# Keeping the pieces of a folded weight in on-chip memory, and a new instruction order

## The chip, the cores and the metric

The kernel runs on one core of a Trainium2 chip. The core has a matrix engine (TensorE, PE; its weight loads are PEld), a vector engine (VectorE, DVE), a scalar engine (ScalarE, ACT), GpSimd (POOL) and SyncE (SP). In this kernel SP does nothing but issue DMAs. SBUF is the on-chip memory that all engines read, PSUM holds matmul results. The metric is the device time of one execution in microseconds, as a median over runs.

## The reference

Three stages follow each other.

```python
# attention, q, k, v: [2, 8, 768, 64], proj: [64, 6]
q_bucket = sum over bits of ((q @ proj) > 0) * 2**bit        # k_bucket the same
scores = where(q_bucket == k_bucket, q @ k.T / sqrt(64), -1e9)
attn = exp(scores - max) / (sum + 1e-9)
x = (attn @ v) as [1536, 512]
# layer 1, d_ff 2048
g = s * relu(x @ w_in)**2 + b
x = g @ w_out
# layer 2, d_ff 1024
h = ((x @ w1) * (x @ w2)) @ w3
out = h @ w_out
```

## The kernel before, in words

All matmuls work on numbers split into a high and a low part in a reduced fp32 format, and take three matmuls (high x high, low x high, high x low), so groups of PE come in threes.

**Attention.** There are 16 heads of 768 queries. `begin` loads q and k of a head, stacked, as t (head 0 in two halves of 384 columns, at L344; others whole, at L347) and v as tv (L348). `q1` is the high part of q and k, `k2` the low part (L395; L456 for head 0). `bits` (L492) multiplies with the projection pj, `mm` (L510) turns the signs into +1 and -1; `q2` and `k1` are rows of q, k and mm copied to other partitions, by a DMA (L381, L466, L477) or, in part for head 0, by a cast (L434 on ScalarE, L436 on VectorE, L437 on GpSimd). Score products `sc` (L529) hold scores and a penalty for each differing bit. VectorE takes the row maxima (L543), ScalarE the exponentials p (L551), PE transposes them (t, L565), ScalarE, VectorE and GpSimd split the transposes into pt (L586 to L607), and PE multiplies with v (o, L571 and L572). L674 and lines near it normalise. `warm` at L502 is a matmul whose result nobody reads; the counts of these groups are in FILLS.

**Layer 1** runs beside attention and behind it: h = x @ w_in, rl and g on ScalarE and VectorE (L828 to L842), then x = g @ w_out, in quarters of d_ff, for both halves of the tokens. Each weight arrives as raw (L717) and is split in six steps by VectorE, ScalarE and GpSimd (L257 to L271). The pieces are saved to DRAM (kept_wi, kept_wo; L737) and reloaded for the second half of the tokens (`again`, L747).

**Layer 2** first folds w3 @ w_out into one matrix whl (`fold`, tiles psw, L1162): for both halves of w3's columns, 8 pieces of w_out (wo2), and 8 of w3 with each. Weights w1 and w2 give seven products of a fast two-by-two scheme (p, L759), which VectorE combines (c, L1132) and multiplies; y (L1203) is the product with whl. Tiles of this stage lie in pools that are opened once attention's are closed; `w2` is the pool of the fold's pieces and of whl, with NW2 buffers of 4 KB a partition.

**What sets the order.** Functions record operations in `Plan` with what each reads and writes. Three tables of constants then fix everything: ORDER gives the order in which all operations are issued (two letters for one), WAYS the engine of each operation that has a choice, PLACES the buffer of each tile. Every engine runs its own operations in that order, and waits by semaphores for what they read and for the buffer that they write.

Of the kernel before, what the change touches and what calls it, by code (L numbers as in the profile page):

```python
# [1263 lines left out]
```

## Time and profile before

| | before |
|---|---|
| median of 3 runs (us) | 741.36 (741.2 to 744.16) |
| the profiled execution (us) | 742.74 |
| its span, first to last instruction (us) | 740.9 |
| PE busy | 729.0 us, 98% |
| VectorE busy | 590.8 us, 80% |
| ScalarE busy | 393.2 us, 53% |
| GpSimd busy | 297.5 us, 40% |
| DMA traffic | 163.03 MB, mean 220 GB/s |

The profile comes from one execution, which took 742.74 us in all; 740.9 of it are the span that the views cut up. Shares of busy time are means over stages with different limits, so stretches and waits say more than the totals.

### The profile page before, as it was taken

The page shows a single profiled execution, that of the slowest core. Times are in us where ns is not written, and L with a number is a line of the kernel's source. Part 1 is how long each engine was busy: PE and PEld are TensorE (multiplying, and loading weights), DVE is VectorE, ACT ScalarE, POOL GpSimd, SP SyncE. Part 2 cuts the span into 40 slices and gives each one's busy share as a digit, 9 for nine tenths or more (in the row PEclk, how much of TensorE's full clock was granted, in tenths as well). Part 3 has the DMA queues.
Part 4 walks back from the last instruction along what each step waited for, and adds up shares of the span by engine and source line. Part 5 has one row for each costly group of instructions (what it writes and reads, how often), then busy time and mean ns, then how long its engine had stood idle before and what let it go on. Part 6 is the DMA issues. An engine that isn't in the chain of part 4 may idle for free.

```text
span 740.9 us, 12707 instructions
## 1 busy us (share of the span) xinstructions
PE 729.0 (98%) x4356; PEld 694.6 (94%) x4356; DVE 590.8 (80%) x1133; ACT 393.2 (53%) x778; POOL 297.5 (40%) x322
## 2 busy tenths in 40 slices
PE   8899999999999999999999999999999999999997
PEld 6889999999999999999999998999998999999996
DVE  7999999999889889999898667665998965664542
ACT  6989989987667667665373432433533312311111
POOL 2698989886565564334230311032125200111000
PEclk9999999999999999999999999999999999999999
DMA  7856557566677477347888996788899998475502
GB/s 217 244 132 175 141 160 194 149 181 171 195 228 236 119 232 255 93 133 254 288 267 298 317 312 242 256 274 290 315 338 315 353 312 261 141 240 186 179 22 86
DMA packets 78592, 163.03 MB, mean 220 GB/s; under 512 B 8896, under 2 KB 46272, under 8 KB 78528
## 3 DMA queue, kind: packets, MB, share of 16 engines
q1 hardware_dynamic: 78528, 162.22, 68.5%
q8 instruction: 35, 0.57, 0.3%
q14 instruction: 29, 0.24, 0.1%
HBM read 103.09 MB, written 41.21 MB: 195 GB/s over the span
## 4 chain that ended last, share of the span: by engine, by line
PE 86%; DVE 7%; DMA 3%; ACT 2%; issue 1%; SPq 0%; DVEq 0%; ACTq 0%
PE x L759 18%; PE h L759 15%; PE p L759 15%; PE y L1203 9%; PE t L565 7%; PE sc L529 7%; PE psw L1162 6%; PE o L571 4%; PE o L572 4%; PE bits L492 2%; DVE sc L543 1%; DVE pt L607 1%; DMA t<-in_qkT 1%; DMA q<-mm 1%; DMA rd<-rq 1%
## 5 line engine op out<-in xcount | busy, mean ns | idle before, releaser
L759 PE MATMUL h<-x,w_wi 128*128 128x384 f32 x768 | 148.1, 338 | 0.0
L759 PE MATMUL x<-g,w_wo 128*128 128x384 f32 x768 | 146.9, 337 | 1.0 <-DVE rl L833 0.9
L759 PEld LDWEIGHTS x<-g,w_wo 128*128 128x128 f32 x768 | 133.6, 188 | 3.6 <-DVE rl L833 1.6
L759 PEld LDWEIGHTS h<-x,w_wi 128*128 128x128 f32 x768 | 133.6, 188 | 2.5 <-DVE pt L607 0.2
L1132 DVE TENSOR_TENSOR c<-c,p 128x384 f32<-128x384 f32 x112 | 60.2, 552 | 57.7 <-PE p L759 54.4
L543 DVE TENSOR_SCALAR_CACHE_REDUCE sc<-sc 128x768 f32<-128x768 f32 x96 | 91.6, 957 | 3.4 <-PE sc L529 2.4
L551 ACT ACTIVATE p<-sc,least 128x768 f32<-128x768 f32 x96 | 86.9, 906 | 11.1 <-DVE sc L543 7.7
L529 PE MATMUL sc<-k,q 128*128 128x384 f32 x384 | 87.0, 347 | 3.0 <-ACT p L551 2.0
L565 PE MATMUL t<-ident,p 128*128 128x128 f32 x576 | 83.9, 273 | 0.2
L759 PE MATMUL p<-x,w 128*128 128x384 f32 x384 | 77.5, 337 | 0.4 <-DVE c L1132 0.3
L571 PE MATMUL o<-pt,vv 128*128 128x256 f32 x288 | 76.9, 295 | 0.1
L572 PE MATMUL o<-pt,vv 128*128 128x256 f32 x288 | 73.1, 282 | 0.0
L565 PEld LDWEIGHTS t<-ident,p 128*128 128x128 f32 x576 | 67.9, 140 | 5.3 <-DVE pt L607 1.5
L759 PEld LDWEIGHTS p<-x,w 128*128 128x128 f32 x384 | 68.0, 188 | 4.5 <-DVE c L1132 1.3
L597 POOL TENSOR_TENSOR pt<-pf,pt 128x512 fp32r<-128x512 f32 x48 | 63.2, 1317 | 21.6 <-ACT pt L593 20.7
L607 DVE TENSOR_TENSOR pt<-t,pt 128x512 fp32r<-128x512 f32 x96 | 65.0, 683 | 6.7 <-ACT pt L603 5.5
L529 PEld LDWEIGHTS sc<-k,q 128*128 128x128 f32 x384 | 64.4, 188 | 5.2 <-ACT p L551 3.0
L603 ACT CAST pt<-t 128x512 fp32r<-128x512 f32 x96 | 56.0, 586 | 16.7 <-PE t L565 7.6
L571 PEld LDWEIGHTS o<-pt,vv 128*128 128x128 f32 x288 | 54.4, 189 | 0.8 <-DVE xf L624 0.3
L572 PEld LDWEIGHTS o<-pt,vv 128*128 128x128 f32 x288 | 54.5, 189 | 0.2
L838 ACT ACTIVATE g<-rl,b_bc 128x384 fp32r<-128x384 f32 x64 | 38.9, 615 | 25.5 <-PE x L759 17.4
L1162 PE MATMUL psw<-w_wo,w_w 128*128 128x512 f32 x192 | 51.6, 394 | 0.0
(263 smaller groups left out, 1271.7 us busy)
## 6 DMA issues: line engine op xcount, KB each, us to landing
w<-kept_s SPq DMA_DIRECT2D x64, 256.0 KB
kept_wo<-w_wo SPq DMA_DIRECT2D x24, 512.0 KB
w_wo<-kept_wo SPq DMA_DIRECT2D x24, 512.0 KB
w<-kept_a SPq DMA_DIRECT2D x48, 256.0 KB
raw_wi<-in_w_in SPq DMA_DIRECT2D x16, 512.0 KB
...
```

What stands on the lines that cost most here:

```text
L529: nc.tensor.matmul(sc()[:, i, :HALF], x[:, t], y[:, i * HALF : (i + 1) * HALF], start=st, stop=not st)
L543: lambda j=j, sc=sc: nc.vector.tensor_scalar(sc()[:, :, :HALF], sc()[:, :, :HALF], OUT, None, ALU.min, ALU.min, accum_out=least()[:, j : j ...
L551: lambda j=j, k=k, sc=sc: nc.scalar.activation(ps[j](), sc()[:, :, :HALF], AF.Exp, bias=least()[:, j : j + 1], scale=-1.0, accum_out=ssum( ...
L565: nc.tensor.transpose(tp()[:, e, j * P : (j + 1) * P], flat[:, c * P : (c + 1) * P], ident)
L571: nc.tensor.matmul(o()[:, :U], w, pt()[:, 0, e], start=(c == 0), stop=False)
L572: nc.tensor.matmul(o()[:, :U], w, pt()[:, 1, e], start=False, stop=(c == NC - 1))
L597: lambda pf=pf, pt=pt: nc.gpsimd.tensor_tensor(pt()[:, 1], pf(), r32(pt()[:, 0]), ALU.subtract),
L607: lambda tp=tp, pt=pt: nc.vector.tensor_tensor(pt()[:, 1], tp(), r32(pt()[:, 0]), ALU.subtract),
L759: nc.tensor.matmul(ps()[:, :n], x, y, start=(i == 0 and e == 0), stop=(i == len(terms) - 1 and e == 2))
L1132: "cadd", "dve", 0.47, rank, lambda: nc.vector.tensor_tensor(x(out), a(), p(), op), [(ps, 1), *reads], writes
L1162: nc.tensor.matmul(ps(), w3()[:, p, c], wo()[:, q], start=(j == 0 and e == 0), stop=(j == 7 and e == 2))
L1203: nc.tensor.matmul(y(), abt()[:, p, c], wt()[:, q], start=(i == 0 and e == 0), stop=(i == DF2 // P - 1 and e == 2))
```

## The change

Three things change.

1. In layer 2 the 8 wo2 pieces are no longer saved to DRAM in half 0 of the fold and reloaded in half 1; the list `wos` keeps them. The pool w2 grows from 14 to 17 buffers.
2. The memory that is set aside for descriptors of GpSimd's DMAs shrinks from 16 to 1 KB a partition, by an argument of the program's constructor.
3. ORDER, WAYS and PLACES are new. Among operations with a choice of engine, six normalisations (L674) and three sums of weights (L1092) go from VectorE to GpSimd. In the first microseconds, the split of the first half of head 0's t goes from ScalarE to VectorE, one cast to q2 from VectorE to GpSimd, another from ScalarE to GpSimd, and one cast to k2 from VectorE to ScalarE. The FILLS groups are 9, 6, 3 and 3 in both; before, the last three stand together.

All line numbers from 986 on are one lower in the changed kernel.

```diff
-NW2 = 14
+NW2 = 17
...
 ORDER = (
-    "AKAAAFABALAGBmXkAMACBnANADX0AEXsAOAbAWAPAVAcAhAXAfAdAUBoAgAQAeAYAZAjAaBvAiXlBuBpAkBwB0DPAqXmAlBsAmArAnB1BqAs"
...
+    "AKALAFABAMAGAABmXkBnANX0AOAVXsACAXAbADAEAfAhAWAPAcAgBoAUAdAYAQAZAeAiAaAjBpBuAkBvXlB0AqBwXmAlDPAnB1ArXnARAmAo"
...
-            whl = [None] * DJ
+            whl, wos = [None] * DJ, []
...
                 for j in range(DJ):
                     if half == 0:
-                        wo = piece(wo2[j // 2], f"wo2_{half}_{j // 2}", j % 2, r + step, late_raw, late_w, ("wo2", j))
-                    else:
-                        wo = again(f"wo2_{half}_{j // 2}", j % 2, ("wo2", j), late_w)
+                        wos.append(piece(wo2[j // 2], f"wo2_{half}_{j // 2}", j % 2, r + step, late_raw, late_w))
+                    wo = wos[j]
                     w3 = piece(w3T[half], f"w3_{half}", j, r - 5 * step, late_raw, late_w)
...
-    nc = bacc.Bacc("TRN2", target_bir_lowering=False, num_devices=1)
+    nc = bacc.Bacc("TRN2", target_bir_lowering=False, num_devices=1, dynamic_dma_scratch_size=1024)
```

Two places show how the order moves.

**The start of the program.** SP's first DMA rows before (t_0 is q and k of head 0, of which each row loads a half; numbers at the end of a name count the tiles):

```order
L344 DMA t_0_229<-in_qkT 128x384
L293 DMA pj_85<-in_projp 128x128
L344 DMA t_0_229<-in_qkT 128x384
L347 DMA t_1_255<-in_qkT 128x768
L717 DMA raw_wi_0_0_0_257<-in_w_in 128x1024
L348 DMA tv_0_259<-in_vl 128x384
L348 DMA tv_1_262<-in_vl 128x384
L717 DMA raw_wi_0_0_2_267<-in_w_in 128x1024
```

SP's first DMA rows now:

```order
L344 DMA t_0_221<-in_qkT 128x384 x2
L348 DMA tv_0_230<-in_vl 128x384
L293 DMA pj_85<-in_projp 128x128
L347 DMA t_1_249<-in_qkT 128x768
L717 DMA raw_wi_0_0_0_251<-in_w_in 128x1024
L348 DMA tv_1_253<-in_vl 128x384
L717 DMA raw_wi_0_0_2_257<-in_w_in 128x1024
L717 DMA raw_wi_0_0_1_263<-in_w_in 128x1024
```

The two halves of t_0 now stand together at the front; tv_0 and pj come behind them, and t_1 fourth as before, behind a tv.

VectorE's rows at the same place before, from the projection's split to the first step of a weight:

```order
L304 TENSOR_TENSOR pj_85<-pj_85,ones_232 128x128
L307 CAST pj_h_86<-pj_85 128x128
L309 TENSOR_TENSOR pj_l_87<-pj_85,pj_h_86 128x128
L456 SCALAR_TENSOR_TENSOR k2_0_272<-t_0_229,qs_71,q1_0_264 128x384
L436 CAST k1_0_275<-q1_0_264 64x384
L456 SCALAR_TENSOR_TENSOR k2_0_272<-t_0_229,qs_71,q1_0_264 128x384
L436 CAST q2_0_283<-q1_0_264 64x384
L510 TENSOR_SCALAR mm_0_291<-bits_0_0_277,thr_75,sgn_76 128x384
L510 TENSOR_SCALAR mm_0_291<-bits_0_1_287,thr_75,sgn_76 128x384
L436 CAST k2_0_272<-mm_0_291 64x384
L260 TENSOR_SCALAR raw_wi_0_0_0_257<-raw_wi_0_0_0_257 128x512
```

VectorE's rows now:

```order
L448 TENSOR_SCALAR q1_0_255<-t_0_221,qs_71 128x384
L456 SCALAR_TENSOR_TENSOR k2_0_259<-t_0_221,qs_71,q1_0_255 128x384
L304 TENSOR_TENSOR pj_85<-pj_85,ones_224 128x128
L307 CAST pj_h_86<-pj_85 128x128
L309 TENSOR_TENSOR pj_l_87<-pj_85,pj_h_86 128x128
L436 CAST k1_0_261<-q1_0_255 64x384
L456 SCALAR_TENSOR_TENSOR k2_0_259<-t_0_221,qs_71,q1_0_255 128x384
L510 TENSOR_SCALAR mm_0_282<-bits_0_0_274,thr_75,sgn_76 128x384
L510 TENSOR_SCALAR mm_0_282<-bits_0_1_284,thr_75,sgn_76 128x384
L395 SCALAR_TENSOR_TENSOR k2_1_303<-t_1_249,qs_71,q1_1_280 128x768
L260 TENSOR_SCALAR raw_wi_0_0_0_251<-raw_wi_0_0_0_251 128x512
```

The first half's split (q1_0) has come to VectorE, ahead of pj. The cast to q2_0, which stood between the second k2_0 and the first mm, and the cast of mm to k2_0 behind the second are gone from it. k2_1 now follows mm directly.

**The first folds, beside layer 1's x_0_2_1.** PE's rows before (h is the product with w_in, w_wo_1_0 a reloaded quarter of w_out, psw the fold; behind a row stands what it waits for, DMAHW3 being a DMA):

```order
L759 MATMUL h_0_3_3_5607<-x0_3_3032,w_wi_1_0_1_5274 128x384 x3
L759 MATMUL h_0_3_3_5607<-x0_3_3032,w_wi_1_0_2_5359 128x384 x3
L759 MATMUL h_0_3_3_5607<-x0_3_3032,w_wi_1_0_3_5384 128x384 x3
L759 MATMUL h_0_3_2_5600<-x0_3_3032,w_wi_1_0_1_5274 128x384 x3
L759 MATMUL h_0_3_2_5600<-x0_3_3032,w_wi_1_0_2_5359 128x384 x3
L759 MATMUL x_0_2_1_5653<-g_0_2_0_5509,w_wo_1_0_0_5563 128x384 [waits DMAHW3_49,DVE_49]
L759 MATMUL x_0_2_1_5653<-g_0_2_0_5509,w_wo_1_0_0_5563 128x384 x2
L759 MATMUL x_0_2_1_5653<-g_0_2_1_5515,w_wo_1_0_1_5440 128x384 x3
L1162 MATMUL psw_0_2_5670<-w_wo2_0_0_0_5336,w_w3_0_0_5521 128x512 x3
L759 MATMUL h_0_3_2_5600<-x0_3_3032,w_wi_1_0_3_5384 128x384 x3
```

PE's rows now:

```order
L759 MATMUL h_0_3_3_5588<-x0_3_2978,w_wi_1_0_2_5351 128x384 x3
L759 MATMUL h_0_3_1_5572<-x0_3_2978,w_wi_1_0_3_5366 128x384 x3
L759 MATMUL h_0_3_2_5595<-x0_3_2978,w_wi_1_0_1_5248 128x384 x3
L759 MATMUL h_0_3_3_5588<-x0_3_2978,w_wi_1_0_3_5366 128x384 x3
L759 MATMUL h_0_3_2_5595<-x0_3_2978,w_wi_1_0_2_5351 128x384 x3
L1161 MATMUL psw_0_2_5638<-w_wo2_0_0_0_5324,w_w3_0_0_5512 128x512 x3
L759 MATMUL h_0_3_2_5595<-x0_3_2978,w_wi_1_0_3_5366 128x384 x3
L759 MATMUL x_0_2_1_5653<-g_0_2_0_5495,w_wo_1_0_0_5541 128x384 [waits DMAHW0_49,DVE_49]
L759 MATMUL x_0_2_1_5653<-g_0_2_0_5495,w_wo_1_0_0_5541 128x384 x2
L759 MATMUL x_0_2_1_5653<-g_0_2_1_5502,w_wo_1_0_1_5424 128x384 [waits DMAHW4_49]
```

The fold psw_0_2 and the last group of h_0_3_2 have moved from behind the first rows of x_0_2_1 to in front of them.

SP's rows that lead up to the reloads for x_0_2_1, before:

```order
L747 DMA w_wo_1_0_1_5440<-kept_wo_0_0_1_158 128x1024
L747 DMA w_wo_1_0_2_5450<-kept_wo_0_0_2_159 128x1024
L737 DMA kept_wo2_0_0_0_185<-w_wo2_0_0_0_5336 128x1024
L717 DMA raw_wo2_0_1_1_5463<-in_wo2 128x1024
L737 DMA kept_wo_0_3_3_184<-w_wo_0_3_3_5142 128x1024
L914 DMA kept_t3_1_224<-t3_0_1_5481 256x1x384
L717 DMA raw_w3_0_1_5545<-in_w3T 128x1024
L747 DMA w_wo_1_0_3_5555<-kept_wo_0_0_3_160 128x1024
L747 DMA w_wo_1_0_0_5563<-kept_wo_0_0_0_157 128x1024
```

SP's rows now:

```order
L717 DMA raw_w3_0_0_5395<-in_w3T 128x1024
L737 DMA kept_wo_0_3_3_184<-w_wo_0_3_3_5135 128x1024
L747 DMA w_wo_1_0_1_5424<-kept_wo_0_0_1_158 128x1024
L717 DMA raw_wo2_0_1_1_5453<-in_wo2 128x1024
L717 DMA raw_w3_0_1_5532<-in_w3T 128x1024
L914 DMA kept_t3_1_216<-t3_0_1_5466 256x1x384
L747 DMA w_wo_1_0_0_5541<-kept_wo_0_0_0_157 128x1024
L747 DMA w_wo_1_0_2_5551<-kept_wo_0_0_2_159 128x1024
L747 DMA w_wo_1_0_3_5558<-kept_wo_0_0_3_160 128x1024
```

The save kept_wo2_0_0_0 is gone; w_wo_1_0_0 now stands ahead of w_wo_1_0_2 and w_wo_1_0_3, one load of raw_w3 and one kept_t behind the last save.

## Rows read from the trace of the kernel before

**Rows 1.** The page, part 1: engine, busy us (share of the span) xinstructions.
```profile
PE 729.0 (98%) x4356; PEld 694.6 (94%) x4356; DVE 590.8 (80%) x1133; ACT 393.2 (53%) x778; POOL 297.5 (40%) x322
```

**Rows 2.** Stretches of the span: each engine's busy us (xinstructions), granted clock, DMA share, GB/s.
```profile
0.00:15.00 15.00, 12.43 (x57) 10.92 (x58) 10.57 (x35) 9.27 (x18) 3.74 (x9) 1.00 0.81 243
15.00:30.00 15.00, 12.39 (x77) 10.15 (x76) 14.19 (x27) 13.55 (x27) 7.11 (x7) 1.00 0.69 195
...
90.00:150.00 60.00, 59.85 (x436) 57.37 (x435) 57.31 (x120) 55.23 (x117) 53.67 (x64) 1.00 0.60 165
...
400.00:525.00 125.00, 125.00 (x660) 117.21 (x659) 86.59 (x151) 44.86 (x78) 24.42 (x25) 1.00 0.83 285
525.00:600.00 75.00, 74.46 (x403) 70.08 (x402) 68.38 (x122) 29.74 (x55) 22.84 (x17) 1.00 0.97 335
```

**Rows 3.** Waits of PE: waiting line <- awaited line: us in total, times, longest.
```profile
PE sc L529 <- ACT p L551: 2.0, 2, 1.2
...
PE bits L492 <- DVE pt L607: 1.0, 1, 1.0
PE x L759 <- DVE rl L833: 0.9, 1, 0.9
...
PE p L759 <- DVE c L1132: 0.3, 1, 0.3
```

**Rows 4.** Timeline of 0 to 31 us: start, duration, engine, line, operation.
```profile
1.64 0.42 SPq L344 DMA_DIRECT2D t<-in_qkT  x1
...
5.90 0.61 ACT L451 ACTIVATE q<-t,qs 128x384 fp32r<-128x384 f32 x1 [2.03 <-DMA t<-in_qkT]
...
7.07 0.92 POOL L386 TENSOR_SCALAR q<-t,qs 128x768 fp32r<-128x768 f32 x1 [5.78 <-DMA t<-in_qkT]
7.20 1.01 DVE L436 CAST q<-q 64x384 fp32r<-64x384 f32 x1
...
7.37 0.38 PE L492 MATMUL bits<-k,pj_h 128*128 128x384 f32 x1
...
8.24 1.26 DVE L510 TENSOR_SCALAR mm<-bits,thr,sgn 128x384 fp32r<-128x384 f32 x2
...
10.26 1.01 DVE L395 SCALAR_TENSOR_TENSOR k<-t,qs,q 128x768 fp32r<-128x768 f32 x1
...
11.79 0.96 DVE L543 TENSOR_SCALAR_CACHE_REDUCE sc<-sc 128x768 f32<-128x768 f32 x1
...
12.83 2.25 PE L502 MATMUL warm<-pj_h 128*128 128x384 f32 x12
...
14.91 0.60 PE L565 MATMUL t<-ident,p 128*128 128x128 f32 x4
```

**Rows 5.** Timeline of 49.5 to 53.5 us, GpSimd and VectorE.
```profile
49.91 1.83 POOL L375 TENSOR_TENSOR k<-t,q 128x768 fp32r<-128x768 f32 x1
...
50.15 1.88 DVE L260 TENSOR_SCALAR raw_wo<-raw_wo 128x512 int32<-128x512 uint32 x1
```

**Rows 6.** Timeline of 372 to 392 us, SP's queue and PE.
```profile
382.47 0.80 SPq L747 DMA_DIRECT2D w_wo<-kept_wo  x2
...
390.76 0.93 PE L759 MATMUL x<-g,w_wo 128*128 128x384 f32 x4 [0.87 <-DVE rl L833]
```

**Rows 7.** Waits of SP's queue, 380 to 395 us.
```profile
SPq L747 <- DMA kept_wo<-w_wo: 1.6, 1, 1.6
```

**Rows 8.** DMA traffic of 375 to 392 us.
```profile
DMA packets 1810, 5.42 MB, mean 319 GB/s; under 512 B 171, under 2 KB 683, under 8 KB 1808
```

**Rows 9.** Groups by line and shape: xcount, busy us, mean ns, idle before.
```profile
L674 POOL TENSOR_TENSOR xf<-rb,xf 128x256 f32<-128x256 f32 x14 | 10.8, 772 | 6.5 <-DMA rb<-rd 6.4
...
L260 DVE TENSOR_SCALAR raw_wo<-raw_wo 128x512 int32<-128x512 uint32 x24 | 12.2, 508 | 1.6 <-DMA raw_wo<-in_wo 1.6
...
L674 DVE TENSOR_TENSOR xf<-rb,xf 128x256 f32<-128x256 f32 x10 | 4.6, 464 | 0.0
```

**Rows 10.** DMA queues: kind, packets, MB, share of 16 engines.
```profile
q1 hardware_dynamic: 78528, 162.22, 68.5%
```

More of the change, by code (lines that the diff above doesn't have):

```diff
@@ new lines @@
+    "AsBqX1ApXtAtX2BsXuA/X3BrXvBtAxAuA8BAAyBxA2EeA9BBByX4AzBUXoA+ASA0AvBzA3BRBVEfATX5DRA4AwXwXpBGDXDSA1BWDYA5BSXq"
+    "BHDTA6B2EgDUXxDVX8A7BTBCX6B3DaBbBDDWGIB5BIB4DQBEBLBJDbB6BFBMCTBcBNXyB7BgCUBXBhDcBKX9DZCVCWBiYMCAX+YUBYBOCXCB"
+    "X/B8BPCyCLBdBZCFCYBQBeCzBaC1B9YAC0BfC2EhBjCGDfEiEnB+C3EoCMCdDgBkDiCeDHL8BlDdElCCCHCZDhCDCNB/EmCOCiDjCaEjCoYB"
+    "D0YNEqDkCbYCCEEpCIEkCfD3D1CJErCgCjC4C8CKD2DICcCPDeCkChC9DJD4ClDKC5C+DBCmEJC6EsGKD5CnDpC/EKDCEMDqCpC7ELGLDDDA"
+    "CqDlYVDrCrDEGMENDmDuGJDFD+DnGRDvEvGSDGD/CQDwGNGTEOD6DsEwCsDoEtEyDLGOExEADtEzL+HYGPCRD7EDEBGQGUFME0D8GVDxCSFN"
@@ new lines @@
+    "AHEPDyETCtEEDzFPEUFEEFCwD9FOCuFQDMECEYEQGWEVHaEGYEFRERDNFrCxE5EZCvFsFuEHEWE6E1EIFtE+EaHbESFvEXDOE2HiEbE/HhE3"
+    "HcGZFwFAFWFFFSEcGaGcFXEuJCE7HdEdGbGdFhHfHZE8E4HkHgGuFTGXFGFbHeFHGYE9FUGeFBHlGvF6HjFYFcGxFCFdHmFZFxGwFDF1FiFV"
+    "GyJEF2FaFyHDFjF3GzFzFkFeGAHEF4GjFIFfHGF7FgGfHFGBJFF8F0F5AJGkHHFlJGF9GgGoJLGCF+GhHpJMHIF/GDG0FJHqGiGpKSFKG9G1"
+    "GqHsFLGlG2HrJHGmHtG4HnIGG5FmJIGnHuIHHoJJGEGrG+YFJOHJIIJKG6JNIJG/G7JPGsHNIKFnJDHSFpHOIlFoGtILH+YGG3JQHzXzImGF"
+    "HKG8H0YHHAKUHPH4FqHLHBIoHQHTH/HCHvInIAHUHMIBKVHRIpHwIQH5KWKcJTHxGGKbIqHVKdH6IMJUHWGHNMKZIRJWH1HXJVKaKXH2JXHy"
@@ new lines @@
+    "KeIVINI6KYH3IbJYJRJoIOKfJSISH7IcJpIvIWITJrH8IXIwI0H9IrJqYIICIPIdIUJsYJIsIeIYIxNOJ9ItIZKgIyI1JZI7AIIaJdJtL9I2"
+    "IuYKJ+IzJeIfKAJaJ/IDI3KTL/JbJiKBI4JuMAMGJjKjMFJfI5JyJkKCJcKkJgO2MBJvKmI8JwKlI9IgJhKnJ3IEKhYcLAJzIFMCKoJlLBJ0"
+    "MDJmKiKDJ4MIMELDI+IjJnK4LCIhKMJ5J1JxMJLEKHMHKELfIkKIKFIiJ2LFMKO4J6YLKJLgKtNNJ7LiKKKNJ8KpKuLjKGNPLVI/KLKqKOKy"
+    "NVLkJAK5KPYdLGJBK6KrKQK7MNLhKvLWKRLKNXNQMOKsKzNWMQLLK0MPLPMRKwQGNRLHMiNSMSMLKxLXMjLYK1MMLMNTK2LIMlLNLQNYNUMk"
+    "LlK3LpNZLRQILJK8LqMmLOL0LmLSLrYWLuLTNaM3LnLsMnLUMcM4LZLoYXMdM6LvYOMTM5MeO5LtLwMXMUO6O/M7LxMYPBMsPALyL1MxM8MV"
@@ new lines @@
+    "NdK9LzYsMZL2LaNeL3NgMtMaNbMWNhNfO7NcYtO8MyMbLbMzK+N6YPL4LcMuMfK/N7MoMgLdO9MvMpMhYuO+N8PCYvMqPDNGNiYYO3N9YQNB"
+    "YwMrL5NCYRYxMwPEN+M0LeNHYDYSM9M1OZNIN/M2NnNDaUOaNsM+RxNyOcNENoTAM/ObNjOdNAQJL6NFNtNJYeQPNkOENuL7NpPHNlNKNqOJ"
+    "OeNLOANzNmPIOFQKPKOKOjPJOLNrPLNvOkQLOGNwN0PcOBQMN1OPOHPFYkOCPMQQQNNxRwOoPdPGYyX7ODYZOIQOOuPfPeaVQTOQOMaWQROf"
+    "QSONPgOlYlQHOgYmOmN2aXOhPxOpOROOYnPhOSYaPyPWOiYoOnYfRyYpP0OqYqPNYgPXQUY0POacPYY1YhOvOrYzRzPRYrY2PSN3OwY3PPY8"
+    "P1YiOTY4Y9PzY+R7R0ZEOxN4OsQXQVP2aMOtY/Y5R6ZFOUPTQYQ0ZAPUY6ZBPrQZOyPQQ1ZGYbZCZMadR5PsY7ZHYjZDZNXrZIaNZOOVZJZP"
@@ L118 @@
+    "3124323o353p364M3q374933213r3825344N3s4O3t39273u3+4P3v4Q4T3w4R4U3x4i4V4j4W4k4X294Z4Y4B4b4c4e4d4f4l4g5W4m4p5l"
+    "4n4J4q4s4r4H4t4w4u564x4K5d4y4z4D6I4+4/5z435A445B3/5s455C5E465X40475F41485Y5G4F5Z5H4E425I5D5a5e5J5b5f5c4A5g5h"
+    "5O5p5i4C5j5k5P5q5m5r5n5t5o5u5w5v5x505y5153525457555K586C596D5+4G5/6P6A6Q6B5U6E6F5M6R4I6G6S6J6H6T6K6U5Q6L5S6M"
+    "5L6N6V6O6Z6a6W6l5R6h6m6b6i6c5V6f6g6n5N6o6r6X6s5T6Y6d6j6e6k6p6q"
 )
 WAYS = (
[L120 removed]
@@ new lines @@
+    "BAABABBABAABABBAABABBABABABABAABABABBAABABABABECBAFDCEAEBDCFABBEFADCBEADCFBEACBCEAFDBCAFECDBAFADFBCEDACDEFBA"
+    "DCBABACBCAABCACBBAAABABABABABBBABABABABADIPABKFGQILNOHKJHCAEGIJMNGJIGIQLHJEACGBMDPNFKJDONMACBACABABAABABABDA"
+    "AHGEHCHGABGCEDGFGADECCHDBACABDBCABACDEFHICGBAHCIDBJFIEAHCBJFDEFCIGHJJBFGAECIICDGEFJBJEAHDIBCBFGJACDHCABGFHCA"
+    "BECHBFAGEFBGCADEHBDCGBCFHEDGFAEBHDCABEFGDBHCGAFEBABABABABABABAABABABAABBBABAABABAABBABABABABABABBABABABBAAAA"
+    "ABBBBABAABBABAABBBABABBBAABBABAABABBAABABAABBABABAABEDBCABCFEBAFFBCDADEBBFDECEAFDFEBABAABABBABAA"
```

151 lines of the change are left out of this document (61 added, 90 removed).

## The prediction

> **What bounds the kernel now.** The page's busy times come first: TensorE (PE) is busy 729.0 of 740.9 us [rows 1]. Cut into stretches, the span shows where the rest lies [rows 2]. From 0 to 15 and from 15 to 30 us PE is busy 12.43 and 12.39 of 15, so 5.2 of its 11.9 idle us are there; from 400 to 525 it is busy all 125.00; the granted clock is 1.00 in each. So the kernel is PE's work plus a few gaps, and a change that leaves the matmuls alone can only close or open gaps. The changed kernel has the same 4356 matmuls, of the same shapes. The time outside the span (742.74 - 740.9 = 1.84) has no part in the change and stays.
>
> The waits of PE name the gaps [rows 3]: ScalarE's exponentials (p) 2.0 us in two waits, VectorE's pt 1.0, VectorE's rl 0.9, VectorE's c 0.3. Three engines feed PE in attention: from 90 to 150 us VectorE is busy 57.31 of 60, ScalarE 55.23, GpSimd 53.67 [rows 2]. There, work moved between them counts even though PE is the bound.
>
> **The change part by part.** *Saves and reloads of wo2.* 16 transfers of 512 KB, 8.4 MB, go; at the 285 GB/s of 400 to 525 us [rows 2] that is 29 us of the queue. The eight reloads lie in half 1 of the fold and save nothing there: PE has no gap from 400 to 525, since pieces arrive before they are wanted. Without that cover a late piece costs its lateness, as the next point shows.
>
> *The gap at 390.* The list puts it to an rl of VectorE, and so does the row of the waiting matmul, x at 390.76 with 0.87 idle [rows 6]. The only rl that ends just then is that of h_0_3_3, which x_0_2_1 doesn't read and which the recorded order issues after x_0_2_1, so PE can't wait for it. The order shows what else its first matmul waits for: a DMA, the reload of w_wo_1_0_0. It is the second of the two that SP issues from 382.47 on (each issue about 0.4), so it took 390.7 - 382.9 = 7.8 us to land: the queue was backed up. SP itself had stood 1.6 us for a save before it could issue them [rows 7]. In that backlog lies the save of the first wo2 piece, which is gone now. At the 319 GB/s of 375 to 392 us [rows 8] its 524 KB took 1.6 us. On PE a fold and h_0_3_2's last group now stand ahead of x_0_2_1 (another fold, psw_0_3, has gone behind it). So 1.6 us of relief stands against a gap of 0.87, about 1.0 with the restart: I take -1.0. The bounds are -1.0 and 0, if another save or an SP wait eats it, since w_wo_1_0_0 is now issued behind raw_w3_0_1 and one kept_t as before.
>
> *The start.* Its timeline is in [rows 4]. The second half of t is issued at 1.64 and ScalarE takes it at 5.90, having idled 2.03. In the changed order it is issued second, one SP issue (0.42) sooner. Then VectorE's cast of q2 (7.20, 1.01 us) stands in front of both mm (8.24, 1.26 together); it goes to GpSimd, and the cast of k2 behind mm goes to ScalarE. The last bits matmul ended at 7.37 + 0.38 = 7.75; less 0.42 is 7.3; one mm is 0.63, so both are done at about 7.9 in place of 9.50, 1.6 sooner. Behind them VectorE does k2 of head 1 (L395), one L260 and one L261 ahead of the first row maximum. Before, k2 started at 10.26 and the maximum at 11.79, 1.5 later, with the L260 ahead of k2; it is now between, another 0.5 [rows 9]. k2 needs GpSimd's L386, which took t_1 at 7.07 for 0.92. t_1 is now issued behind a tv, some 0.4 later: 7.5 + 0.9 = 8.4, and 8.4 + 1.5 + 0.5 = 10.4 for the maximum, 1.4 sooner. GpSimd's first cast (at most 1.0, by VectorE's row) is done before t_1 lands. The transposes (14.91) follow. Between 1.2 (all of that cast in the way) and 1.6 **I take -1.4**. The bounds: 0, if the feeding engines give the lead back, and -2.4, if half of the 2.0 us of later exponential waits [rows 3] goes too, since these hang on the same row maxima.
>
> *The fills* (L502). Before, 12 stand in a row (2.25 us) and the transposes begin as they end [rows 4]. Now 6 stand there, and two groups of 3 (0.6 each by that row) between score products of head 0, where PE waits up to 1.2 us [rows 3]. 0, or +0.6 for each group whose wait is gone.
>
> *Ways.* Six normalisations (L674) and three weight sums go from VectorE to GpSimd. A normalisation takes 464 ns on VectorE and 772 on GpSimd [rows 9]: the six make VectorE 2.8 us lighter and GpSimd 4.6 heavier. By the order only one or two of them lie ahead of 150 us, where both are full. I take 0; bounds -0.9 (two normalisations off VectorE) and +2.4 (two collisions like the next).
>
> A collision stands at 50.15 [rows 5]: L260 takes 1.88 us, where 24 of them average 508 ns [rows 9], while GpSimd's k<-t,q runs from 49.91 to 51.74; it ends 0.29 behind it, and PE then waits 1.0 for pt. Which instructions meet hangs on timing: this meeting may go and another come, so I count it unchanged. [...]
>
> *525 to 600.* The first loads of layer 2 stand in a queue 0.97 busy, and PE is idle 75 - 74.46 = 0.54, 0.3 of it for c [rows 2, 3]. With 8.4 MB less ahead, and three more buffers, loads are issued earlier. Bounds 0 and -0.54; I take -0.3.
>
> *1 KB for descriptors.* The 162.22 MB of the kernel's own transfers are on the hardware queue q1 [rows 10], issued by SP; no DMA of GpSimd's uses the space: 0.
>
> **Sum.** -1.4 - 1.0 - 0.3 = -2.7 us: span 740.9 -> 738.2, own time 742.74 -> 740.0. The profiled execution lies 1.4 above the median of 741.36, so the median should be **738.7**. A half per cent, about what a measurement here can tell from no change, is 3.7 us: faster means under 737.65, slower over 745.07.
>
> **Rivals.** *More is gained.* The meeting at 50 goes (1.0) and half of the exponential waits with it (1.0): -4.7, 736.7. For it: VectorE loses work up to 150 us. Against: it was busy 14.19 of 15 between 15 and 30 [rows 2], and its row maxima set the exponentials. Chance 0.25.
> *The lead comes to nothing*, with the reload at 390 late by another wait: 0 to -1, so 740.9. For it: from 90 to 150 the feeding engines are as full as PE, so that a lead of PE's at 30 may be used up by waiting for them. Against: PE has no wait for them on the list between 60 and 390. Chance 0.18.
> *Slower: GpSimd.* It is 89% busy from 90 to 150 [rows 2] and gets more, and each of its longer instructions can hold up VectorE's as at 50. The price is 1.0 a time for PE, with VectorE full. Three of them eat the gain; seven give -2.7 + 7 = +4.3, 745.7. One in 741 us was seen. [...] Chance 0.07.
> The forecast's own case (-1.8 to -4) has 0.5.
>
> **Range.** The low end lies beyond the second case with all the bounds but the meeting at 50: -2.4 - 1.0 - 0.54 - 0.9 = -4.8, and 0.8 for that meeting's part, 735.8. The high end is a loss of 1: 742.4. About 0.2 lies outside. Faster by over 0.5% is the second case and the lower edge of the forecast's: 0.25 + 0.06 = 0.31; slower 0.06; else 0.63. The forecast's own range is 737.4 to 739.6.
>
> **What would show it.** Right: PE busy some 13 of the first 15 us or first transposes near 13.5; mm done near 8; no wait of x between 375 and 395; half 1 of the fold without a gap. Wrong: new waits of PE for pt or p between 45 and 150, a layer-1 reload late somewhere else, GpSimd above 55 of 60 from 90 to 150 with VectorE's pt (L607) longer. The prediction fails if gaps move instead of closing: the sum treats them as separate, while they share VectorE.

## The result, and the profile after

| | before | after |
|---|---|---|
| median (us) | 741.30 (740.42 to 744.16, 6 runs) | 745.51 (745.18 to 746.03, 6 runs) |
| ratio, 95% interval | | 1.0052 [1.0035, 1.0068] |
| the profiled execution, its span (us) | 742.74, 740.9 | 745.73, 743.9 |

The change makes the kernel slower by about 4 us. The forecast was 738.7, and 742.4 the upper end of its range.

The page, part 1 (engine, busy us, share, instructions), beside [rows 1]:

```profile
PE 729.7 (98%) x4356; PEld 695.1 (93%) x4356; DVE 597.0 (80%) x1123; ACT 391.8 (53%) x780; POOL 311.9 (42%) x330
```

PE's work is the same. VectorE does ten instructions fewer than before and is busy 6.2 us longer: some of them must have become longer. The stretches, as in [rows 2]:

```profile
0.00:15.00 15.00, 9.86 (x48) 8.79 (x48) 11.20 (x35) 9.19 (x17) 5.40 (x11) 1.00 0.83 247
15.00:30.00 15.00, 13.80 (x75) 12.09 (x75) 13.55 (x24) 10.61 (x20) 8.98 (x8) 0.89 0.66 170
90.00:150.00 60.00, 59.81 (x436) 57.61 (x436) 57.33 (x120) 55.04 (x116) 53.08 (x64) 1.00 0.61 165
525.00:600.00 75.00, 72.50 (x387) 67.07 (x386) 69.26 (x117) 29.69 (x57) 24.40 (x19) 1.00 0.94 324
```

Two stretches got worse. From 0 to 15 us PE is busy 9.86 where it was 12.43; from 15 to 30 it is busy longer than before with two matmuls fewer, because the granted clock is 0.89 there (0.66 from 15 to 20, with 0.50 from 16 to 19): the matmuls of bits that start 0.17 us apart at 12.40 start 0.32 apart at 15.68. From 525 to 600 it is busy 72.50 where it was 74.46. The stretch of GpSimd and VectorE that the prediction feared, 90 to 150, is as it was. The waits of PE, as in [rows 3]:

```profile
PE t L565 <- ACT p L551: 1.9, 1, 1.9
...
PE p L759 <- DVE c L1131: 1.4, 2, 0.8
PE bits L492 <- DVE pt L607: 1.0, 1, 1.0
PE x L759 <- DVE rl L833: 0.9, 1, 0.9
PE bits L492 <- DVE k L395: 0.8, 1, 0.8
PE bits L492 <- DVE k L456: 0.7, 1, 0.7
PE bits L492 <- DVE pj_h L307: 0.7, 1, 0.7
```

The wait of x for rl reads like the one in [rows 3], but it is another one: the wait at 390.76 [rows 6] is gone, and a new one stands at 536.59, below. The wait for pt is the old meeting of [rows 5], 1.9 us later. Three waits of bits are new, and all lie in the first 27 us. The timeline of the start, beside [rows 4]:

```profile
5.46 0.29 DVE L304 TENSOR_TENSOR pj<-pj,ones 128x128 f32<-128x128 f32 x1 [1.07 <-DMA pj<-in_projp]
...
6.06 0.44 PE L492 MATMUL bits<-q,pj_h 128*128 128x384 f32 x1 [0.66 <-DVE pj_h L307]
...
6.73 0.91 POOL L386 TENSOR_SCALAR q<-t,qs 128x768 fp32r<-128x768 f32 x1 [1.97 <-DMA t<-in_qkT]
6.76 1.29 DVE L456 SCALAR_TENSOR_TENSOR k<-t,qs,q 128x384 fp32r<-128x384 f32 x1
...
7.97 1.29 DVE L510 TENSOR_SCALAR mm<-bits,thr,sgn 128x384 fp32r<-128x384 f32 x2
...
10.49 2.44 POOL L375 TENSOR_TENSOR vv<-tv,vv 128x384 fp32r<-128x384 f32 x2 [1.27 <-ACT vv L368]
10.57 1.49 DVE L261 SCALAR_TENSOR_TENSOR raw_wi<-raw_wi 128x512 int32<-128x512 int32 x1
11.36 1.20 PE L502 MATMUL warm<-pj_h 128*128 128x384 f32 x6
11.98 0.95 DVE L543 TENSOR_SCALAR_CACHE_REDUCE sc<-sc 128x768 f32<-128x768 f32 x1
...
14.99 0.66 PE L565 MATMUL t<-ident,p 128*128 128x128 f32 x4 [1.91 <-ACT p L551]
```

VectorE waits 1.07 us for pj, whose load now stands fourth in SP's queue. L456 and, ahead of the first maximum, L261 are drawn out beside instructions of GpSimd (0.62 and 0.69 alone). mm is done at 9.26, 0.24 sooner than before, where 1.6 was predicted; the maximum comes at 11.98, not at 10.4. The load of t_1 is now the fifth, not the fourth as the part on the change says; GpSimd's L386 took it at 6.73, sooner than the 7.07 of [rows 4], so this branch held nothing up. The six fills and three matmuls of bits end at 13.1, and PE then waits 1.91 us for p.

Three places of layer 2 follow (lines of GpSimd, VectorE and PE; those that play no part are left out):

```profile
533.62 1.83 POOL L1091 TENSOR_TENSOR raw_w_a<-raw_w_a,raw_w_a 128x512 f32<-128x512 f32 x1 [0.81 <-DVE w_w_a L271]
533.98 2.02 DVE L271 TENSOR_TENSOR w_w_s<-raw_w_a,w_w_s 128x512 fp32r<-128x512 f32 x1
535.93 1.13 DVE L833 SCALAR_TENSOR_TENSOR rl<-h,sw,rl 128x384 f32<-128x384 f32 x2
...
536.59 8.61 PE L759 MATMUL x<-g,w_wo 128*128 128x384 f32 x48 [0.87 <-DVE rl L833]
...
561.14 1.64 POOL L270 TENSOR_TENSOR w_w_a<-raw_w_a,w_w_a 128x512 fp32r<-128x512 f32 x1
561.52 1.81 DVE L267 SCALAR_TENSOR_TENSOR raw_w_a<-raw_w_a 128x512 int32<-128x512 int32 x1
563.25 1.20 DVE L1131 TENSOR_TENSOR c<-c,p 128x384 f32<-128x384 f32 x2
563.85 2.38 PE L759 MATMUL p<-x,w 128*128 128x384 f32 x12 [0.62 <-DVE c L1131]
...
592.56 1.31 POOL L270 TENSOR_TENSOR w_w_s<-raw_w_a,w_w_s 128x512 fp32r<-128x512 f32 x1 [3.40 <-ACT w_w_s L268]
592.61 1.81 DVE L261 SCALAR_TENSOR_TENSOR raw_w_a<-raw_w_a 128x512 int32<-128x512 int32 x1
594.34 1.01 DVE L1131 TENSOR_TENSOR c<-c,p 128x384 f32<-128x384 f32 x2
594.94 0.79 PE L759 MATMUL p<-x,w 128*128 128x384 f32 x3 [0.76 <-DVE c L1131]
```

At 534, 561 and 593 the same happens: a preparation of weights on VectorE (0.69 alone) starts while a GpSimd instruction runs, takes 1.8 to 2.0 us, and behind it in VectorE's order stands an rl or a c that PE wants. PE stands idle 0.87, 0.62 and 0.76 us; counted from the start of one matmul to the start of the next, less the usual step, it loses 1.03, 0.78 and 0.93 (called its loss below). Two of the three GpSimd instructions (534 and 561) were VectorE's before the change. Beside another long GpSimd instruction (1.91 us from 553.66), a c at 554.09, which reads p from PSUM, keeps its usual 0.55.

### The profile page after: what moved, and what is told of

Same layout as the page of the kernel before. It is cut to its first block, busy times and chain, and to the rows that moved or that the text cites. A ratio compares the mean times of both kernels' runs of the same rounds, so it can differ in the third digit from the quotient of the medians.

```text
span 743.9 us, 12702 instructions
## 1 busy us (share of the span) xinstructions
PE 729.7 (98%) x4356; PEld 695.1 (93%) x4356; DVE 597.0 (80%) x1123; ACT 391.8 (53%) x780; POOL 311.9 (42%) x330
## 4 chain that ended last, share of the span: by engine, by line
PE 90%; DVE 5%; ACT 1%; DMA 1%; issue 1%; POOL 1%; SPq 0%; DVEq 0%; POOLq 0%; ACTq 0%
PE x L759 18%; PE h L759 18%; PE p L759 15%; PE y L1202 8%; PE sc L529 8%; PE t L565 7%; PE psw L1161 6%; PE o L572 4%; PE o L571 4%; PE bits L492 2%; DVE sc L543 1%; DVE pt L607 1%; DMA kept_a<-w_w_a 1%; ACT p L551 1%; DVE c L1131 0%
## 5 line engine op out<-in xcount | busy, mean ns | idle before, releaser
L1131 DVE TENSOR_TENSOR c<-c,p 128x384 f32<-128x384 f32 x112 | 60.3, 552 | 58.1 <-PE p L759 57.2
L543 DVE TENSOR_SCALAR_CACHE_REDUCE sc<-sc 128x768 f32<-128x768 f32 x96 | 91.8, 958 | 5.8 <-PE sc L529 5.0
L597 POOL TENSOR_TENSOR pt<-pf,pt 128x512 fp32r<-128x512 f32 x48 | 63.6, 1325 | 30.4 <-ACT pt L593 20.6
L607 DVE TENSOR_TENSOR pt<-t,pt 128x512 fp32r<-128x512 f32 x96 | 65.1, 682 | 6.1 <-ACT pt L603 4.9
L828 ACT ACTIVATE rl<-h 128x384 f32<-128x384 f32 x64 | 31.2, 491 | 44.8 <-PE h L759 36.0
```

Of the source, the lines that this page charges most:

```text
L543: lambda j=j, sc=sc: nc.vector.tensor_scalar(sc()[:, :, :HALF], sc()[:, :, :HALF], OUT, None, ALU.min, ALU.min, accum_out=least()[:, j : j ...
L597: lambda pf=pf, pt=pt: nc.gpsimd.tensor_tensor(pt()[:, 1], pf(), r32(pt()[:, 0]), ALU.subtract),
L607: lambda tp=tp, pt=pt: nc.vector.tensor_tensor(pt()[:, 1], tp(), r32(pt()[:, 0]), ALU.subtract),
L1131: "cadd", "dve", 0.47, rank, lambda: nc.vector.tensor_tensor(x(out), a(), p(), op), [(ps, 1), *reads], writes
```

## The experiments

All are timed against the kernel before, whose median was between 740.7 and 741.2 in each batch (741.3 beside the changed kernel). Medians of different batches therefore compare to about half a microsecond, and where it matters the difference of the ratios, times 741 us, is given too. Edits are shown as rows of the order or of the table of engines. Theories: **A**, the loss is in VectorE's preparations beside GpSimd's instructions, in layer 2 and at the start; **B**, keeping the pieces costs something, in buffers or memory; **C**, the start alone loses.

**Keeping alone** (e2). Before's ORDER and WAYS, pieces kept, 17 buffers, 1 KB.

```diff
 NW2 = 17
-ORDER, WAYS, PLACES of the change
+ORDER, WAYS of before, without the 8 saves and 8 reloads of wo2
```

> The kernel before with only the pieces kept, 17 buffers and 1 KB for descriptors; its own order and its own choice of engines, without the 8 saves and 8 reloads, and a new placement inside that one pool. Meetings: keeping is harmless; 740 to 741.5, with the gap near 390 us smaller or gone (-0 to -1). Memory (the kept pieces, the smaller descriptor space or the pool cost the time): 743 or more.

740.57 us (739.62 to 741.96), ratio 0.9994 [0.9984, 1.0004]. B falls: it expected 743 or more. PE's gap at 390 is gone in its trace, with the order otherwise as before, so keeping is what closes it; what that is worth (-1.0 predicted) is within what these runs can tell from nothing.

**Three instructions back on VectorE** (e1), those of the three places above.

```diff
-POOL L1091 (534), POOL L270 (561), POOL L270 (593)
+DVE  L1091,       DVE  L271,       DVE  L271
```

> The changed kernel with three operations given back to VectorE: one sum of weights (its GpSimd form starts at 533.6 us) and the low parts of two pieces (561.1 and 592.6). Each of the three ran beside a VectorE instruction that took 2.02, 1.81 and 1.81 us in place of 0.69, and PE then stood 1.03, 0.78 and 0.93 us. Meetings (VectorE and GpSimd hold each other up): the three gaps shrink by 2 us or more, time 742.5 to 743.5; VectorE does 2.1 us more work but loses 3.6 us of stretching. Order (the new order asks VectorE for more around 535 to 595 us than it can do, whoever holds it up): the gaps stay, 745 to 746.

743.85 us, 1.0037 [1.0024, 1.0051]: 1.7 less than after (1.1 by the ratios, whose intervals overlap), between the numbers of the two theories. The three losses shrink to 0.29, 0.27 and 0.41, by 1.8 in all, and one of 0.96 stands at 264, where layer 1's x waits for an acc of VectorE. That is a meeting too: ahead of the acc L260 takes 1.23 us, where 0.42 is usual (timeline of e1):

```profile
261.83 1.83 POOL L375 TENSOR_TENSOR k<-t,q 128x768 fp32r<-128x768 f32 x1
262.71 1.23 DVE L260 TENSOR_SCALAR raw_wo<-raw_wo 128x512 int32<-128x512 uint32 x1 [1.51 <-DMA raw_wo<-in_w_out]
```

Up to there e1 is the same program as after, where this L260 runs at 262.20, ahead of GpSimd's L375 at 263.15, and takes 0.47. So this loss is no effect of the edit: in one order a meeting comes or goes with a microsecond or two between executions.

**All of before's engines in the changed order** (e4).

```diff
-WAYS of the change
+WAYS of before
```

> The changed kernel (kept pieces, new order, new places) with every choice of engine of the kernel before. Meetings: two of the three GpSimd operations that met VectorE in layer 2 are back on VectorE, so about 1.8 us less there, 743 to 744.5, unless new meetings arise. Order: 745 to 746, with the same gaps from 535 to 595 us.

758.39 us, 1.024 [1.0221, 1.0259], which no theory had. PE waits longest for VectorE's pt (h, 5.7 us in three waits), and from 150 to 300 us it is busy 143.23 of 150. An order and its table of engines belong together here; taking the whole table back says nothing about the change. What makes VectorE late there is open.

**Halves of the change** (e5 to e8). Before's and the changed order with their engines, joined at 33 us or at 362 us. All four keep the pieces.

```diff
 e5: before to 33 us, changed from there    e6: changed to 33 us, before from there
 e7: changed to 362 us, before from there   e8: before to 362 us, changed from there
```

> Up to about 33 us the order, the engines and the places of the kernel before, behind it those of the changed kernel; pieces kept, all work done. Two places (the start and the meetings in layer 2 cost about the same): the start no longer loses, 742 to 743.5, with the three gaps of PE from 535 to 595 us still there. Layer 2 alone (a lead at the start is given back before 400 us): 745 to 746.

> The reverse: up to about 33 us the changed kernel's order and engines, behind it those of the kernel before with the pieces kept (alone: 740.6). Two places: the start's loss of 2 to 3 us is carried to the end, 742.5 to 743.5. Layer 2 alone: 740 to 741.

> The changed kernel's order and engines up to about 362 us (attention and half of layer 1), those of the kernel before from there on, pieces kept. Two places: without the meetings at 534, 561 and 593 us about 2.5 less than the changed kernel, 742.5 to 743.5. Start alone: 745 to 746.

> The kernel before with the pieces kept up to about 362 us, the changed kernel's order and engines from there on. Two places: the gaps of PE near 534, 561 and 593 us come with it, 742.5 to 743.5, as the two halves' losses should add up to the 4.9 us between 740.6 and 745.5. Timing only (the meetings hang on what happened before, so they don't come): 740 to 741.

e5 744.16, 1.0037 [1.0024, 1.0049]; e6 741.83, 1.0007 [0.9998, 1.0015]; e7 742.41, 1.0017 [1.0008, 1.0026]; e8 743.57, 1.0033 [1.0021, 1.0046]. So the part from 362 us on costs 743.57 - 740.57 = 3.0 (and 745.51 - 742.41 = 3.1 with the rest changed; by the ratios 2.9 and 2.6); the intervals of each pair are apart. The changed start costs 741.83 - 740.57 = 1.3 (745.51 - 744.16 = 1.35; by the ratios 1.0 and 1.1); it is seen twice, but the intervals of each pair overlap. That is half of what was expected of it, so e5 and e6 lie between the numbers of their two theories. For 33 to 362 us e7 less e6 and e5 less e8 give 0.6 each, also within overlapping intervals; in e5's trace PE waits 0.98 us at 262 for the acc of the meeting that e1 shows at 264, in that of after it does not. Each part costs about the same whichever order stands beside it, so the costs add up, and C falls. In e8 the three gaps stand at 532, 560 and 591 with losses of 1.04, 0.78 and 0.92, 2.7 of the 3.0; in e6 and e7 there are none.

**Two moved instructions alone** (e9), on e2, to see whether a meeting costs by itself.

```diff
-DVE  L1091 raw_w_0_1_a    DVE  L271 w_w_1_0_a
+POOL L1091 raw_w_0_1_a    POOL L270 w_w_1_0_a
```

> Only two instructions move from VectorE to GpSimd (the L1091 sum and the L270 difference of the second layer that the change moved), in the order of before with the pieces kept. Theory A, a meeting by itself costs: each puts an instruction on GpSimd beside VectorE's preparation of weights, TensorE gets gaps near 530 and 560 us of about 1.0 and 0.8 us, and the time goes from 740.6 to 741.5 to 742.4. Rival B, the order decides which instruction of VectorE is beside it: in this order nothing that TensorE waits for stands behind, no gap over 0.5 us, and the time stays within 740.0 to 741.0.

740.74 us, 0.9994 [0.9985, 1.0002]: the numbers of rival B. The first meeting takes place all the same (timeline of e9):

```profile
530.70 1.79 POOL L1091 TENSOR_TENSOR raw_w_a<-raw_w_a,raw_w_a 128x512 f32<-128x512 f32 x1 [3.81 <-issue]
531.45 1.59 DVE L271 TENSOR_TENSOR w_w_s<-raw_w_a,w_w_s 128x512 fp32r<-128x512 f32 x1 [0.35 <-ACT w_w_s L268]
532.96 0.61 DVE L833 SCALAR_TENSOR_TENSOR rl<-h,sw,rl 128x384 f32<-128x384 f32 x1
```

but L271 starts 0.4 us later in GpSimd's instruction, and PE's loss at rl is 0.48. So B's reason, that nothing which PE waits for stands behind, does not hold here: rl does, and PE has more slack. The second meeting does not take place: at 557.64 VectorE's L267 starts ahead of GpSimd's L270 and takes 0.81. The moved engines cost little in the old order; in the new order around them they cost more.

**The same meetings, VectorE's part moved** (e12), on e8: GpSimd's instructions stay, three preparations go behind the rl or c.

```diff
+DVE L833 rl, L833 rl      +DVE L1131 c          +DVE L1131 c
 DVE L271 w_w_s (531)       DVE L267 raw (559)    DVE L261 raw (590)
-DVE L833 rl, L833 rl      -DVE L1131 c          -DVE L1131 c
```

> Before up to 362 us, then the changed order, with GpSimd's instructions left where the change put them, and three preparations of weights on VectorE (those that took 2.0, 1.8 and 1.8 us at 531, 559 and 590 us) issued one or two instructions later, behind the rl and the two c that TensorE waits for. Theory A, the loss is only that a drawn-out instruction stands ahead of one that TensorE waits for, and instructions that read PSUM (rl, c) keep their length beside GpSimd: the three gaps of 1.0, 0.8 and 0.9 us go, and the time goes from 743.6 to 740.8 to 741.6. Rival B, whatever stands beside GpSimd's instruction is drawn out, rl and c too: the gaps stay near 0.8 us each and the time within 743.0 to 744.0.

741.80 us, 1.0011 [1.0002, 1.002]: 1.8 less than e8 (1.6 by the ratios, and the intervals are apart), between the theories' numbers. The first and third gap are gone, and rl keeps its length beside GpSimd, 1.14 us for two where after's two at 535.93, beside none, take 1.13 (timeline of e12):

```profile
531.06 1.84 POOL L1091 TENSOR_TENSOR raw_w_a<-raw_w_a,raw_w_a 128x512 f32<-128x512 f32 x1 [0.81 <-DVE w_w_a L271]
532.13 1.14 DVE L833 SCALAR_TENSOR_TENSOR rl<-h,sw,rl 128x384 f32<-128x384 f32 x2 [0.62 <-ACT rl L828]
533.19 0.68 DVE L271 TENSOR_TENSOR w_w_s<-raw_w_a,w_w_s 128x512 fp32r<-128x512 f32 x1
...
561.01 0.69 DVE L271 TENSOR_TENSOR w_w_a<-raw_w_a,w_w_a 128x512 fp32r<-128x512 f32 x1 [0.58 <-ACT w_w_a L268]
561.62 1.48 DVE L1131 TENSOR_TENSOR c<-c,p 128x384 f32<-128x384 f32 x3
562.68 0.62 PE L759 MATMUL p<-t_again,w 128*128 128x384 f32 x2 [0.81 <-DVE c L1131]
```

The second came back as another wait: L267 at 559.27 keeps its 0.69, ScalarE's cast of it starts at 560.32 (behind a DMA, by the profile), and VectorE's next L271 stands idle 0.58 for that cast, ahead of a c that PE wants. A shows as the mechanism in layer 2: with GpSimd's instructions where they were, moving VectorE's out of the way gives back 1.8 of the 3.0. One place mended made another.

**The old meeting at 50 us** (e10), on e2: L260 five VectorE instructions later (the fifth is the read that follows L543).

```diff
-DVE L260 raw_wo
 DVE L543 sc, L607 pt, L607 pt, L624 xf
+DVE L260 raw_wo
```

> The order of before with the pieces kept, in which the one L260 on raw_wo at 48.6 us (1.87 us long there beside GpSimd's k<-t,q) is issued five VectorE instructions later. Theory A, TensorE's gap of 1.2 us at 50.7 is the length of that one instruction ahead of the pt that TensorE waits for: the gap goes, and the time goes from 740.6 to 739.2 to 739.8. Rival B, another instruction that works on SBUF alone is drawn out in its place, or the chain waits for something else: 740.2 to 741.2 with a gap of the same size.

739.70 us (738.98 to 740.38), 0.9978 [0.9968, 0.9987], 0.9 below e2 (1.2 by the ratios): the numbers of A. The gap is gone; L607 keeps 0.69 beside k<-t,q (timeline of e10):

```profile
49.60 1.84 POOL L375 TENSOR_TENSOR k<-t,q 128x768 fp32r<-128x768 f32 x1
50.96 0.69 DVE L607 TENSOR_TENSOR pt<-t,pt 128x512 fp32r<-128x512 f32 x1
```

L260 itself, at 53.14, takes 0.53. This is the one version whose interval lies below the kernel before: the pieces kept, its old order, and one instruction moved.

**The start** (e3, e11, e13 to e15, e17, e18): e3 on the changed kernel, the others on e6.

```diff
 e3:  pj's load second in SP's queue       e11: 12 fills, not 6, ahead of the first t
 e13: both                                 e14: VectorE's L261 behind the maxima, ScalarE's L264 behind L261
 e15: e13, e14 and e10                     e17: e13, L261 behind the maxima, L264 behind both p
 e18: e17 and e10
```

> The changed kernel with one DMA moved: pj is issued second on SP, between the two halves of t_0, as before, in place of fourth. Late pj: the split of pj begins near 3.5 us in place of 5.46, the first bits near 5 in place of 6.06, the first transposes about 1 us sooner than 14.99; if that lead is kept to the end 744.5, otherwise 745.5 with the lead lost between 100 and 400 us. Meetings elsewhere unchanged: the gaps from 535 to 595 stay in either case.

> The changed start, then the order of before, with the two last groups of fills (3 and 3 matmuls) moved forward to stand behind the first two groups' end, ahead of the first transposes. Theory A, the changed start loses because TensorE stands idle longer before the transposes and its clock falls behind that: with fills there the profile shows no stretch at half the clock between 14 and 20 us, and the time goes from 741.8 to 740.9 to 741.4. Rival B, the loss is in the late pj and in VectorE's and GpSimd's instructions beside each other, which the fills don't change: 741.5 to 742.1.

> The changed start, then the order of before, with pj's load issued second on SP's queue and all twelve fills ahead of the first transposes. Theory A, late pj and idle TensorE with the half clock behind it make the start's loss together (each mended alone left the other): no stretch at half the clock between 7 and 20 us, and the time goes from 741.8 to 740.4 to 741.1. Rival B, the loss is in VectorE's L261 beside GpSimd's L375 and what follows: 741.4 to 742.1.

> The changed start, then the order of before, with VectorE's L261 at 10.5 us (1.5 us long there beside GpSimd's L375) and the ScalarE instruction that reads its result issued behind the first two maxima. Theory A, its length stands ahead of the maxima and so of the first p: the first transposes come about 0.8 to 1.4 us earlier than at 15.0 us, and the time goes from 741.8 to 740.6 to 741.2. Rival B, the chain is held elsewhere (pj, the clock): 741.5 to 742.1.

> The changed start with the edits of both other kernels (pj second, fills together, L261 behind the maxima), then the order of before with L260 on raw_wo behind at 50 us. Theory A, the changed start with these mended is worth what was predicted of it: below the 739.7 of the order of before with the L260 behind alone, 738.3 to 739.3. Rival B, mended it is only as good as the start of before: 739.4 to 740.2. Rival C, the start's loss is elsewhere: 740.4 to 741.2.

> The changed start with pj second, the fills together, VectorE's L261 behind the first two maxima and ScalarE's L264 behind the first two p; then the order of before. Theory A, L261 stood ahead of the maxima and L264's wait was the miss of the other run: the first p begins at about 12.0 us, the first transposes at 13.9 to 14.2 us, and the time goes from 740.9 to 739.8 to 740.5. Rival B, the start is held by pj and the clock alone: 740.5 to 741.5.

> The same start, and L260 on raw_wo behind at 50 us. Theory A, the start of the change is worth something when mended: 738.6 to 739.4, below the 739.7 of before's start with the same L260. Rival B, it is worth as much as that of before: 739.4 to 740.2. Rival C, worse: over 740.2.

e3 744.21 (742.22 to 747.67), 1.005 [1.0031, 1.007], the ratio of the changed kernel: the first transposes come 1.1 us sooner, at 13.93, as expected, and the time doesn't follow. e11 741.91, 1.0009 [1.0, 1.0018], as e6 and in rival B's range. e13 740.90 (739.68 to 744.81), 1.001 [0.9997, 1.0022]: the median lies in A's range, the ratio is that of e6. e14 745.26, 1.0056 [1.0044, 1.0068], worse than e6 by 3.4; e15 741.11, 1.0006 [0.9996, 1.0017], rival C; e17 741.84 (738.64 to 744.14), 1.0003 [0.9987, 1.0019], above the ranges of both theories; e18 741.41 (739.2 to 744.72), 1.0003 [0.9989, 1.0017], rival C.

e14's timeline shows a miss of the edit, and what a longer wait of PE costs there:

```profile
14.68 0.70 ACT L264 ACTIVATE raw_wi<-raw_wi 128x512 f32<-128x512 f32 x1 [3.50 <-DVE raw_wi L261]
...
17.19 0.72 PE L565 MATMUL t<-ident,p 128*128 128x128 f32 x4 [2.81 <-ACT p L551]
...
18.67 1.48 PE L529 MATMUL sc<-k,q 128*128 128x384 f32 x4
```

L264 stood ahead of p and waited 3.50 us for L261. The transposes come at 17.19, and behind them the matmuls run at a lower clock (granted 0.58 from 17 to 21 us, 1.00 from 14 to 17): four score matmuls take 1.48 us, where e2's take 0.96. e17 mends that. In its profiled execution (740.22) mm is done at 7.81 and the first maximum starts at 9.55, both as early as predicted or earlier, and the first transposes begin at 12.57, 1.75 us before e2's 14.32. The lead does not last. First e2's lines and its row from 15 to 25 us, then e17's:

```profile
14.32 0.60 PE L565 MATMUL t<-ident,p 128*128 128x128 f32 x4
14.68 0.96 PE L529 MATMUL sc<-k,q 128*128 128x384 f32 x4
...
15.00:25.00 10.00, 8.44 (x54) 7.19 (x52) 9.87 (x19) 9.57 (x18) 3.72 (x4) 1.00 0.67 180
```

```profile
12.57 0.65 PE L565 MATMUL t<-ident,p 128*128 128x128 f32 x4
...
16.24 0.66 PE L565 MATMUL t<-ident,p 128*128 128x128 f32 x4 [1.03 <-DVE mm L510]
...
15.00:25.00 10.00, 7.71 (x49) 6.48 (x48) 10.00 (x19) 8.65 (x17) 5.80 (x5) 1.00 0.76 192
```

VectorE is busy 9.87 and 10.00 of 10 there, and PE waits 1.03 us for its mm: in these two executions VectorE, not PE, bounds the stretch, and an earlier PE waits for it. In e18's profiled execution (743.97) the same stretch is another one:

```profile
15.00:25.00 10.00, 7.49 (x28) 5.82 (x26) 7.68 (x13) 5.53 (x11) 3.33 (x3) 0.66 0.65 167
```

The granted clock is 0.66 (0.68 from 15 to 20 us, 0.64 from 20 to 25). The trace of after shows the values 1.00 and 0.50 (16 to 19 us); if e18's clock took the same two, about two thirds of the stretch lay at the lower one, by estimate. Ahead of the stretch PE had stood idle 1.24 us, up to 14.09. Executions of e17 and e18 differ by 5.5 us, those of e10 by 1.4. Much of that goes with the clock. Of all 35 executions of e13, e17 and e18, the nine with a mean granted clock of 0.994 to 0.998 took 742.0 to 744.8 us (743.8 on average), the 26 at 0.999 or 1.000 took 738.6 to 742.8 (740.8 on average). In e6 the lower clock cost nothing that shows: four executions at 0.997 took 741.9 on average, the seven at 0.999 or 1.000 took 741.8. So the mended start gains in its best executions (738.64, where e2's best is 739.62) and loses in others, and the median with e10's edit, 741.41, is no better than the 739.70 of before's start with it. By the ratios none of the mends can be told from e6 (1.0007), but for e14, which is worse: which of the start's waits carry its loss stays open.

**All mends in the changed order** (e16): the start as in e15, L260 behind at 54 us, VectorE's preparations behind at 534 and 593, one L270 back on VectorE.

```diff
+the edits of e15; e12's first and third; e1's second
```

> The changed order throughout, with the three edits of the start, L260 on raw_wo behind at 54 us, VectorE's preparations at 534 and 593 us behind the rl and c that TensorE waits for, and the one GpSimd difference at 561 us back on VectorE. Theory A, these places account for nearly all that the change lost and for one loss of before too: 745.5 less 1.3, 0.9, 1.0, 0.6 and 0.9 gives 740.8, within 740.0 to 741.6. Rival B, mended waits come back elsewhere, as they did at 561 us: 742.0 to 744.0.

744.34 us, 1.0047 [1.0034, 1.006]: above even rival B's 742.0 to 744.0, and B's mechanism. The gaps in layer 2 and that at 54 us are gone, but PE now loses 1.7 us at 63, where VectorE's L387, beside GpSimd's L597, takes 1.55 us ahead of a pt that PE wants, and 1.2 at 264, where L260 takes 1.92 ahead of the acc, in the meeting of e1; and the start still carries e14's miss. All edits together gave 1.2 us by the medians (745.51 to 744.34) and 0.4 by the ratios, whose intervals nearly coincide.

## Why the prediction was wrong, step by step

The kernel is 6.8 us slower than predicted, and 6.0 of it lie in two terms of the sum, the start (2.7) and 525 to 600 (3.3). The prediction itself named the way in which it would fail, and it is what happened: gaps moved instead of closing, and the new ones hang on VectorE.

**The gap at 390: right.** It is gone with the saves and reloads, in after and in e2 alike, so it hung on them and not on the rl that the row names; that it was the landing of w_wo_1_0_0 in particular rests on the order of the rows. Its worth of 1.0 can't be separated from nothing in e2's interval (-0.0016 to +0.0004, -1.2 to +0.3 us).

**"The start. I take -1.4": failed.** It measured +1.3 (e6 against e2; +1.0 by the ratios). The step followed t's second half through ScalarE and mm and left out two things that its own order rows showed. First, pj's load went from second to fourth in the queue; VectorE takes it at 5.46 us, and in e2 at 3.50, so the first bits wait for it. Second, the durations were those of instructions with no GpSimd instruction running ahead of them: L456 and L261 are drawn out by 0.67 and 0.80 in the new order. These waits are seen in the trace; that they make up the 1.3 was not shown, since e13, which removes those of pj and L456, and e17, which removes all three, have ratios like e6's. And a deeper step failed, the one from a lead of PE to a shorter time: e17's profiled execution had the lead that was predicted, and VectorE, full from 15 to 25 us, used it up. That is the rival "the lead comes to nothing", though it looked for the full engines from 90 to 150 us; the row that told was there before, with VectorE at 14.19 of 15 from 15 to 30 [rows 2]. Why the start is worse than before's, and not only no better, stays open.

**"525 to 600, -0.3": failed, at +3.0** (e8 against e2). The step looked at loads only, and took the order of VectorE and GpSimd in this stretch as it was. In the new order three preparations of VectorE meet instructions of GpSimd ahead of what PE waits for, 1.0 + 0.8 + 0.9.

**"Ways. I take 0": mis-placed rather than mis-sized.** The bound of +2.4 was for normalisations ahead of 150 us, and that stretch is unchanged. One of the sums of weights, named in the change and given no place, met at 534. The L270 that met at 561 is not among the nine moves at all: these are what is left when instructions are counted line by line, while 156 of the 509 entries of WAYS differ, and this one was VectorE's L271 before. By e9 the two moved instructions alone cost 0.2, within the noise; with the changed order around them they are part of the 3.0.

**The rival "Slower: GpSimd"** had the right mechanism and price (1.0 a time; measured 0.8 to 1.0 in layer 2 and 0.9 at 50), in the wrong stretch. It asked for seven meetings, since it set them against a gain of 2.7. That gain did not come, and three meetings with the start's loss beside them were enough. A chance of 0.07 was too small for the one thing that a new order moves everywhere.

**Taken at 0, and right:** the fills (e11: 0.1); the 1 KB and the buffers (e2); wo2's transfers (8.4 MB gone, no time that e2 could tell from nothing). The meeting at 50, counted as unchanged, is there again with a loss of 1.18; that was luck, since the one at 264 came in e1 and e16 and not in after, in the same order.
